# Cross-window attention on one core: an order of work kept as strings, single PSUM banks, and most products on GpSimd in halves

## The chip, the core and the metric

The kernel runs on one core of one Trainium2 chip. Times are device microseconds of that core for one launch. A core has five engines that run side by side, each with its own queue of instructions taken strictly in order: TensorE (PE, matmuls; PEld is its loading of weights), VectorE (DVE), ScalarE (ACT, here the exponentials), GpSimd (POOL) and SyncE (SP, here the queue that starts the transfers). They meet through semaphores. TensorE writes only to PSUM, which has eight banks of 512 fp32 columns over 128 partitions.

## The reference

A picture of 224 x 224 positions with 96 channels is projected to queries, keys and values. The first 48 channels attend within horizontal stripes of 8 rows, the other 48 within vertical stripes of 8 columns; each stripe has 1792 positions. The two results are put side by side and projected.

```python
qkv = jnp.einsum('bhwc,cd->bhwd', x, wqkv)          # x: 1,224,224,96; C2 = 48
q, k, v = qkv[..., :C], qkv[..., C:2*C], qkv[..., 2*C:]
qh, kh, vh = (t[..., :C2].reshape(28, 8*224, C2) for t in (q, k, v))
ah = softmax(einsum('bqc,bkc->bqk', qh, kh) * C2**-0.5)
oh = einsum('bqk,bkc->bqc', ah, vh)
# the same for t[..., C2:], with stripes of 8 columns: ov
out = einsum('bhwc,cd->bhwd', concat(oh, ov), wo)
```

So there are 56 stripes, each with a score matrix of 1792 x 1792, all of which goes through an exponential.

## The kernel before, in words

**Pairs of stripes.** The 56 stripes are worked two at a time: 28 pairs P, 14 of horizontal and then 14 of vertical ones (`NPH`). The two stripes of a pair (`w`) lie in the two halves of the partitions. Queries come in four chunks of columns (`CH`: 512, 512, 512, 256), keys in 14 tiles of 128. A *unit* is one key tile (two for the last chunk) against one chunk of queries, for both stripes: two banks of scores, 128 x 1024. A pair has 49 units. There are 28 x 49 = 1372.

**Two ways to the exponential.** Of each chunk, `NDC` = 3, 2, 2, 2 units go through VectorE (`d_units`, 252) and the rest through ScalarE (`a_units`, 1120):
- ScalarE, line 773: one ACTIVATE with Exp over two banks, out to a buffer `PT` (eight of them); then PV matmuls (line 738) on `PT`.
- VectorE: line 801 brings the scores to int16 (`I_sb`, 128 x 1024 for a unit, two units to a buffer of 2048). For two units together, line 813 makes `U_sb` and line 815 `E_sb`, bit operations over 2048 columns. Line 820 multiplies `I_sb` and `U_sb` to `G_sb`, one instruction for each unit. The exponential is `E` + `G`, so such a unit has two PV steps, one on each. A product is made on VectorE, or on GpSimd where the planner chose that.

**The rest.** Line 518 projects queries and keys, lines 529 and 535 bring them to SBUF; line 547 (on GpSimd; line 546 on VectorE for the first pair) takes the mean off the keys; lines 573 and 578 make the values. After a chunk's last PV, line 702 copies its sum to `OT_sb`, lines 618 and 653 project it, lines 606 and 658 take the reciprocal, lines 625 and 662 divide. For vertical stripes line 666, on GpSimd, adds the horizontal stripes' part (`Ph_sb`), and line 675 stores on SyncE's queue, which also loads x (line 412) and stores the horizontal part (line 639).

**What sets the order.** The program is not written out: a planner (`Planner`) runs when the kernel is built. It has a list of queues (*streams*) for each engine and a price for each operation (`occ`, the time for which it holds the engine, and `lat`, the time to its result), and always places the operation that can start first by these prices, with a rule of its own for TensorE (`pick_pe`), which weighs score matmuls (mode `q`) against all others (mode `v`). `emit` then writes each engine's instructions in the placed order with waits on semaphores. On the chip only the order is fixed; when each starts is set by its waits. A *lock* keeps the planner from placing GpSimd's work and VectorE's operations 813, 815 and 820 at one time; it is a price in the plan and no wait on the chip.

**PSUM.** Three pairs of banks (0-1, 2-3, 4-5: `ring`) hold scores. Banks 6 and 7 (`obanks`) collect PV sums of the live chunks. Projections (`fill`) take a free bank of 6 and 7, or one half of a score pair (`FillPool`).

The few lines that tell how a product comes to GpSimd before:

```python
def choose(op):
    work = sum(o_.occ for q_ in (dve_ot, dve_d1, dve_ev) for o_ in q_ if all(...))
    for g in gs:
        if work >= WANT and pl.t["pool"] <= op.start + 1.0:
            g.eng, g.occ, g.lat = "pool", 2.12, 2.2
            pool_v.append(g)
```

Of the kernel before, what the change touches and what calls it, by code (L numbers as in the profile page):

```python
# [26 lines left out]

class Op:
    __slots__ = ("eng", "occ", "lat", "fn", "deps", "soft", "alloc", "then", "wait", "tok", "dma", "mode", "start", "end", "lock")

    def __init__(s, eng, occ, lat, fn, deps=(), soft=(), alloc=(), then=None, dma=None, mode=None):
        s.eng, s.occ, s.lat, s.fn, s.deps, s.soft, s.alloc, s.then = eng, occ, lat, fn, list(deps), list(soft), list(alloc), then
        s.wait = s.start = s.end = None
        s.tok, s.dma, s.mode, s.lock = {}, dma, mode, eng == "pool"
# [38 lines left out]
SWITCH = 0.10  # L73


class Planner:
# [21 lines left out]
    def ready(s, op):  # L98
        t = 0.0
        for d in op.deps:  # L100
            if d.end is None:
                return None
            if not (d.eng == "pe" and op.eng == "pe"):
                t = max(t, s.when(d, op.eng))
# [13 lines left out]
    def place(s, op, t):  # L118
        deps = list(op.deps)
        for pool, name, n in op.alloc:  # L120
            ks = pool.peek(lambda o: s.when(o, op.eng), n)[1]
            deps += pool.take(ks)
            op.tok[name] = ks[0] if n == 1 else sorted(ks)
# [26 lines left out]
    def n_q(s, t):  # L150
        return sum(1 for w, _ in s.ring.order(lambda o: s.when(o, "pe")) if w <= t + EPS)

    def pick_pe(s, cands):
        t = s.t["pe"]
        run_end = max(s.t["act"], t) + 0.903 * s.pend
        C = []
        for r, prio, q in cands:
            C.append((max(r, t + (SWITCH if q[0].mode != s.mode else 0.0)), prio, q))
        if any(c[1] == PRIO[0] for c in C) and run_end - t < DRUN:
            C = [c for c in C if c[1] != PRIO[1]]  # L160
        V = [c for c in C if c[2][0].mode == "v"]
        Q = [c for c in C if c[2][0].mode == "q"]
        now = t + EPS
        first = min(C, key=lambda c: (c[0], c[1]))
        if s.mode == "q":
            q_now = [c for c in Q if c[0] <= now]
            if q_now:
                return min(q_now, key=lambda c: c[1])
            v_now = [c for c in V if c[0] <= now + SWITCH]
            q_soon = [c for c in Q if c[0] <= t + HOLD]  # L170
            if q_soon:
                return min(q_soon, key=lambda c: c[0])
            if v_now:
                return min(v_now, key=lambda c: c[1])
            return first
        v_now = [c for c in V if c[0] <= now]
        q_now = [c for c in Q if c[0] <= t + SWITCH + EPS]
        need = SWITCH + 0.46
        if v_now:
            c = min(v_now, key=lambda c: c[1])  # L180
            if q_now:
                if t + c[2][0].occ > run_end - need:
                    return min(q_now, key=lambda c: c[1])
                if t > run_end - RUN and s.n_q(t + SWITCH) >= BATCH:
                    return min(q_now, key=lambda c: c[1])
            return c
        if q_now and (s.n_q(t + SWITCH) >= BATCH or t + 0.25 > run_end - need):
            return min(q_now, key=lambda c: c[1])
        return first

    def run(s):
        while True:
            best = None
            for e, streams in s.streams.items():
                cands = []
                for prio, q in streams:
                    if q:
                        r = s.ready(q[0])
                        if r is not None:
                            cands.append((r, prio, q))  # L200
                if not cands:
                    continue
                if e == "pe":
                    c = s.pick_pe(cands)
                else:
                    cands = [(max(r, s.t[e]), p, q) for r, p, q in cands]
                    m = min(c[0] for c in cands)
                    c = min((c for c in cands if c[0] <= m + 0.03), key=lambda c: c[1])
                if best is None or c[0] < best[0]:
                    best = c  # L210
            if best is None:
                break
            s.place(best[2].popleft(), best[0])
# [10 lines left out]
EPS, HOLD, RUN, BATCH = 0.05, 0.12, 1.2, 1  # L224
PRIO = (1, 0, 3, 5, 4, 2)
WANT = 0.8
NEAR, LEAD, SPACE, PACE, DRUN, FIRST = 1, 8, 3, 0.9, 1.0, 0


def bass_standalone__window_attn_cswin__vision_kernel(  # L230
# [27 lines left out]
    with es:  # L258
# [31 lines left out]
        def two(s):  # L290
            return ps3[:, 2 * s:2 * s + 2, :]
# [14 lines left out]
        dve_ot, dve_d1, dve_ev, dve_ts = (pl.stream("dve", i) for i in range(4))  # L306
# [3 lines left out]
        ring = Pool([0, 1, 2])  # L310
        obanks = Pool([6, 7])
        pl.ring = ring
# [4 lines left out]
        class FillPool:  # L317


            def __init__(s):  # L320
                s.pair, s.half = None, {}

            def peek(s, when, n):
                near = any(k.left <= NEAR for k in live) or len(live) != 1
                got = obanks.order(when)
                if got and not near:
                    return (got[0][0], [got[0][1]])
                opt = []
                for k, f in s.half.items():
                    if f is not None and all(o.end is not None for o in f):  # L330
                        opt.append((max([when(o) for o in f], default=0.0), k))
                if s.pair is None:
                    opt += [(t, 2 * p) for t, p in ring.order(when)]
                opt.sort()
                opt = opt or got
                return (opt[0][0], [opt[0][1]]) if opt else None

            def take(s, ks):
                k = ks[0]
                if k >= 6:  # L340
                    return obanks.take(ks)
                if s.pair is None:
                    s.pair = k // 2
                    deps = ring.take([s.pair])
                    s.half = {k: None, k ^ 1: deps}
                    return deps
                deps, s.half[k] = s.half[k], None
                return deps

            def free(s, k, by):  # L350
                if k >= 6:
                    obanks.free(k, by)
                    return
                s.half[k] = list(by)
                if s.half[k ^ 1] is not None:
                    ring.free(s.pair, s.half[k] + s.half[k ^ 1])
                    s.pair, s.half = None, {}
        fills = FillPool()
# [236 lines left out]
        def out_war(P):  # L595

            assert P < 2 or len(out_dma[P - 2]) == 8
            return out_dma[P - 2][-1:] if P >= 2 else []

        def fin(P, c):  # L600
# [7 lines left out]
            if is_h[P]:  # L608
                bcs = list(range(q0 // 64, (q0 + qs) // 64))
                for i in range(0, len(bcs), 4):  # L610
# [17 lines left out]
                    def rel(op, rop=rop):  # L628
# [3 lines left out]
                                   ("dve", 0.07 + 0.1 * n, d2, out_war(P), True, dve_ev, [], rel)], stream=pe_fin)  # L632
# [10 lines left out]
            else:  # L643
                for w in range(2):
# [28 lines left out]
                    def done(op, w=w, j=j, hold=hold):  # L673
# [9 lines left out]
                                   ("pool", 0.95, d3, out_dma[NPH - 2][-1:] + out_dma[NPH - 1][-1:] + out_war(P), False, pool_o, [], done)],  # L683
                                  stream=pe_fin)
                    hold += ops[:2]
                    fin_pe[P].append(p)
# [4 lines left out]
        def pv_done(k, op):  # L691
# [12 lines left out]
            def then(ev):  # L704
                obanks.free(k.bank, [ev])
# [7 lines left out]
        class OTPool:  # L713
# [3 lines left out]

            def peek(s, when, n):
# [4 lines left out]
                return obanks.peek(when, 1)  # L723

            def take(s, ks):
# [4 lines left out]
                return obanks.take(ks)  # L730

        def pv_op(k, kts, lhs, rhs, deps, then):
            q0, qs = CH[k.c]

            def fn(e):
                for i, kt in enumerate(kts):
                    for w in range(2):
                        ins = e.matmul(bank(k.bank)[64 * w:64 * w + 64, 0:qs], lhsT=lhs(w, kt), rhs=rhs(w, i, qs),  # L738
                                       start=(op.tok["first"] and i == 0), stop=(k.last is op and i == len(kts) - 1))
# [6 lines left out]
            op = Op("pe", 0.222, 0.40, fn, deps, [], [(OTPool(k), "o", 1)], placed, mode="v")  # L746
            return op

        def qk(e, u, s):
# [3 lines left out]
            for i, kt in enumerate(kts):  # L753
                for w in range(2):
                    ins = e.matmul(bank(2 * s + w)[:, i * qs:(i + 1) * qs], lhsT=KT_sb[b][64 * w:64 * w + C2, kt * 128:(kt + 1) * 128],  # L755
                                   rhs=QT_sb[b][64 * w:64 * w + C2, q0:q0 + qs], start=True, stop=True)
            return ins

        def add_a(i, u):
# [6 lines left out]
            q = Op("pe", 0.222, 0.40, None, [k_early[P] if kts[-1] < 2 else k_ready[P], q_ready[(P, c)]], [], [(ring, "s", 1)], q_then, mode="q")  # L766
            q.fn = lambda e: qk(e, u, q.tok["s"])
# [4 lines left out]
            a = Op("act", 0.903, 1.023, None, [q], [], [(pts, "p", 1)], act_then)  # L772
# [14 lines left out]
        n_d = [0]  # L787
        held = []

        def add_d(u, soft):  # L790
# [4 lines left out]
            q = Op("pe", 0.222, 0.40, None, [k_early[P] if kts[-1] < 2 else k_ready[P], q_ready[(P, c)]], soft, [(ring, "s", 1)], mode="q")  # L795
            q.fn = lambda e: qk(e, u, q.tok["s"])
# [153 lines left out]
```

## Time and profile before

| | before |
|---|---|
| median of 3 runs | 1052.47 us |
| lowest, highest | 1051.34, 1058.28 us |
| the profiled execution: its time | 1050.19 us |
| its span, first to last instruction | 1048.3 us |
| granted TensorE clock | 0.998 |
| exponentials on ScalarE (line 773) | 1120 |
| units on VectorE (line 801) | 252 |
| products on VectorE, on GpSimd (line 820) | 224, 28 |

The page of a profile gives busy time of each engine and its share of the span, the chain of work that ended last, and groups of instructions, with the mean time of one and the idle time of the engine ahead of them. For ScalarE and VectorE the time of one instruction counts from its dispatch, which can come while the one before still runs; the pace is then read from a row of the chain, which gives a stretch and how many instructions it holds. In a row of the timeline stand the start, the duration, the engine, the line, the operation, and in brackets the idle time ahead of it and what ended it.

### The profile page before, as it was taken

How to read it: one execution, taken by the hardware profiler on the slowest of the kernel's cores; microseconds unless marked ns; L12 is line 12 of the kernel's file. 1: busy time of each engine (PE TensorE's matmuls, PEld its weight loads, DVE VectorE, ACT ScalarE, POOL GpSimd, SP SyncE). 2: the span in 40 equal slices, each digit the busy share in tenths (PEclk: the TensorE clock that was granted, in tenths of full speed). 3: DMA queues.
4: the chain of work that ended last, by engine and by line, in shares of the span. 5: the costliest groups of instructions: out<-in, count | busy, mean ns of one | idle time of the engine just before them, and what ended most of it. 6: DMA issues, size and time to landing. Idle time of an engine off the chain costs nothing.

```text
span 1048.3 us, 25024 instructions
## 1 busy us (share of the span) xinstructions
PE 1021.6 (97%) x10602; PEld 383.7 (37%) x10602; DVE 964.5 (92%) x1772; ACT 1031.1 (98%) x1128; POOL 234.3 (22%) x171
## 2 busy tenths in 40 slices
PE   8999999999999999999999999999999999999997
PEld 2333333333333333333333333333333333333332
DVE  6999988999998989999999999999999999999896
ACT  6999999999999999999999999999999999999997
POOL 0211011000011100100114434343316323213352
PEclk9999999999999999999999999999999999999999
DMA  6133334342313334231542122122212212212011
GB/s 109 37 28 53 46 28 63 50 49 28 63 36 36 46 45 64 28 51 24 54 61 46 43 46 54 35 47 51 44 33 54 51 31 51 48 43 37 16 25 29
DMA packets 191368, 46.69 MB, mean 45 GB/s; under 512 B 191256, under 2 KB 191256, under 8 KB 191256
## 3 DMA queue, kind: packets, MB, share of 16 engines
q1 hardware_dynamic: 190664, 45.04, 27.1%
q8 instruction: 83, 1.36, 0.6%
q14 instruction: 29, 0.24, 0.1%
q10 hardware_dynamic: 592, 0.06, 0.0%
HBM read 0.10 MB, written 9.63 MB: 9 GB/s over the span
## 4 chain that ended last, share of the span: by engine, by line
ACT 97%; DVE 1%; PE 1%; DMA 0%; SPq 0%; issue 0%; ACTq 0%; POOL 0%; POOLq 0%; DVEq 0%
ACT PT L773 97%; DMA xT_sb<-in_x_dram 0%; PE ps L755 0%; SPq L421 0%; PE ps L738 0%; DVE KT_sb L535 0%; DVE V_sb L578 0%; SPq L412 0%; DVE I_sb L801 0%; DVE KT_sb L546 0%; ACTq L258 0%; POOL out_sb L666 0%; POOLq L258 0%; PE ps L653 0%; PE ps L518 0%
## 5 line engine op out<-in xcount | busy, mean ns | idle before, releaser
L773 ACT ACTIVATE PT<-ps 128x1024 bf16<-128x1024 f32 x1120 | 1027.5, 1271 | 2.7 <-PE ps L755 2.7
L755 PE MATMUL ps<-QT_sb,KT_sb 48*128 48x512 bf16 (+1 forms) x3136 | 476.7, 357 | 15.6 <-ACT PT L773 5.4
L738 PE MATMUL ps<-PT,V_sb 128*64 128x512 bf16 (+1 forms) x2520 | 394.9, 364 | 1.2 <-ACT PT L773 1.0
L801 DVE TENSOR_SCALAR I_sb<-ps 128x1024 int16<-128x1024 f32 x252 | 307.3, 1220 | 26.6 <-PE ps L755 24.7
L755 PEld LDWEIGHTS ps<-QT_sb,KT_sb 48*128 48x128 bf16 x3136 | 130.1, 93 | 357.9 <-ACT PT L773 273.6
L666 POOL TENSOR_TENSOR out_sb<-tmp,Ph_sb 112x384 bf16<-112x384 f32 x112 | 121.3, 1093 | 250.2 <-DVE tmp L662 235.0
L738 PEld LDWEIGHTS ps<-PT,V_sb 128*64 128x64 bf16 x2520 | 119.4, 108 | 129.0 <-issue 115.5
L820 DVE TENSOR_TENSOR G_sb<-I_sb,U_sb 128x1024 bf16<-128x1024 bf16 x224 | 163.9, 744 | 0.3
L547 POOL TENSOR_SCALAR KT_sb<-KT_sb,negmean 128x1792 bf16<-128x1792 bf16 x27 | 53.9, 1995 | 319.3 <-DVE kjunk L540 282.0
L820 POOL TENSOR_TENSOR G_sb<-I_sb,U_sb 128x1024 bf16<-128x1024 bf16 x28 | 59.3, 2122 | 241.9 <-DVE E_sb L815 241.9
L738 PE MATMUL ps<-G_sb,V_sb 128*64 128x512 bf16 (+1 forms) x616 | 97.3, 350 | 0.4 <-DVE G_sb L820 0.4
L738 PE MATMUL ps<-E_sb,V_sb 128*64 128x512 bf16 (+1 forms) x616 | 89.9, 351 | 0.8 <-DVE E_sb L815 0.2
L813 DVE TENSOR_SCALAR U_sb<-I_sb 128x2048 int16<-128x2048 int16 x126 | 88.1, 699 | 0.2
L815 DVE TENSOR_SCALAR E_sb<-I_sb 128x2048 int16<-128x2048 int16 x126 | 86.1, 683 | 0.0
L518 PE MATMUL ps<-xT_sb,w_sb 96*64 96x512 bf16 x448 | 79.8, 366 | 2.0 <-DMA xT_sb<-in_x_dram 1.5
L702 DVE CAST OT_sb<-ps 128x512 bf16<-128x512 f32 x112 | 69.3, 619 | 11.0 <-PE ps L738 10.6
L535 DVE TENSOR_SCALAR_CACHE_REDUCE KT_sb<-ps 128x512 bf16<-128x512 f32 x110 | 67.7, 619 | 12.0 <-PE ps L518 11.4
L529 DVE TENSOR_SCALAR QT_sb<-ps 128x512 bf16<-128x512 f32 x110 | 66.8, 616 | 7.4 <-PE ps L518 7.0
L662 DVE TENSOR_TENSOR tmp<-ps,rc 112x384 f32<-112x384 f32 x112 | 62.0, 554 | 1.9
L578 DVE CAST V_sb<-ps 128x480 bf16<-128x480 f32 (+1 forms) x112 | 55.6, 499 | 6.1 <-PE ps L573 6.0
L625 DVE TENSOR_TENSOR out_sb<-ps,rc 128x384 bf16<-128x384 f32 x98 | 54.2, 553 | 1.2
L573 PE MATMUL ps<-w_sb,xT_sb 96*64 96x48 bf16 x1568 | 43.9, 191 | 0.0
(32 smaller groups left out, 309.5 us busy)
## 6 DMA issues: line engine op xcount, KB each, us to landing
Ph_sb<-out_sb SPq DMA_DIRECT2D x112, 84.0 KB, 4.4
out_dram<-out_sb SPq DMA_DIRECT2D x112, 84.0 KB, 1.9
xT_sb<-in_x_dram SPq DMA_TRANSPOSE x254, 2.4
wo_sb<-in_wo_dram SPq DMA_DIRECT2D x4, 9.0 KB
wo_sb<-one_sb SPq DMA_DIRECT2D x4, 0.0 KB
w_sb<-in_wqkv_dram ACTq DMA_DIRECT2D x1, 54.0 KB, 3.4
xT_sb<-in_x_dram SPq DMA_DIRECT2D x2, 3.0 KB, 3.7
```

Of the source, the lines that this page charges most:

```text
L518: ins = e.matmul(bk[64 * w:64 * w + 64, 0:qs], lhsT=w_sb[0:C, wblk(P, kind), :], rhs=rhs, start=True, stop=True)
L529: return e.tensor_scalar(dst, src, A128, None, ALU.mult)
L535: return e.tensor_scalar(dst, src, 1.0, None, ALU.mult, ALU.add, accum_out=acc)
L666: return e.tensor_tensor(out_sb[b][0:HB, :, w, 2 * c:2 * c + 2, :].rearrange("p h d c -> p d h c"), tmp[hold[1].tok["t"]][0:HB, 0:n, :].re ...
L702: return e.tensor_copy(OT_sb[b][:, q0:q0 + qs], bk[:, 0:qs])
L738: ins = e.matmul(bank(k.bank)[64 * w:64 * w + 64, 0:qs], lhsT=lhs(w, kt), rhs=rhs(w, i, qs), start=(op.tok["first"] and i == 0), stop=(k.l ...
L755: ins = e.matmul(bank(2 * s + w)[:, i * qs:(i + 1) * qs], lhsT=KT_sb[b][64 * w:64 * w + C2, kt * 128:(kt + 1) * 128], rhs=QT_sb[b][64 * w: ...
L773: a.fn = lambda e: e.activation(PT[a.tok["p"]][:].rearrange("p (s n) -> p s n", s=2), two(q.tok["s"]), ACTF.Exp, scale=LN128)
L801: d.fn = lambda e: e.tensor_scalar(I_sb[d0.tok["y"]][:, j * 1024:(j + 1) * 1024].rearrange("p (s n) -> p s n", s=2), two(q.tok["s"]), 128. ...
L813: f.fn = lambda e: e.tensor_scalar(U_sb[y()][:, :], I_sb[y()][:, :], M_FRAC, HALF, ALU.bitwise_and, ALU.bitwise_or)
L815: x2.fn = lambda e: e.tensor_scalar(E_sb[x2.tok["l"]][:, :], I_sb[y()][:, :], M_EXP, E_LOW, ALU.bitwise_and, ALU.bitwise_or)
L820: g.fn = lambda e, i0=i0, i1=i1: e.tensor_tensor(G_sb[x2.tok["l"]][:, i0:i1], I_sb[y()][:, i0:i1].bitcast(BF16), U_sb[y()][:, i0:i1].bitca ...
```

## The change

The planner's own choices of order, of banks and of products for GpSimd go, and five strings, `PLAN`, take their place. `pe`, `dve` and `pool` name, for each instruction of TensorE, VectorE and GpSimd, the queue that is served next (`forced`). For TensorE: 0 warming up, 1 scores for ScalarE, 2 scores for VectorE, 3 PV of `E` and `G`, 4 PV of `PT`, 5 projections of results, 6 projections of x. For VectorE: 0 set-up, 1 copies of line 702, 2 line 801, 3 other copies and divisions, 4 lines 813, 815 and 820. For GpSimd: 1 key updates, 2 products, 3 additions. `far` has one bit for each product: 1 sends it to GpSimd, as two halves of 512 columns. `bank` says where each result goes in PSUM: a digit is a bank; scores take that bank and the next, all else the one bank. All eight banks lie in one pool. ScalarE and SyncE are planned as before.

The strings' counts: `pe` 3560 characters (18 zeros, 1120 ones, 252 twos, 504 threes, 1120 fours, 210 fives, 336 sixes), `dve` 1464, `pool` 535 (27 ones, 396 twos, 112 threes), `far` 252 (198 ones), `bank` 2030. The planner's prices still tell when it places what, but no longer the order within these three engines. Also changed: the prices of the exponential and of a change of mode, and an addition or a division that follows stores now waits for all eight of them (`late`). Code for fused score and PV matmuls (`place2`, `weave`) and for line 801 in halves (`HALVES`) is there and isn't reached: no string holds w, x, y or z, and `HALVES` is False.

```diff
+PLAN = {
+    "pe": (
+        "00000000000000000066666666111662641421461411423613412641341261341431641166331441254144124163134164411363315414"
...
+    "far": (
+        "11110111101111111110100101110011101010111111111011101001011001111111111111111110011110110111110110111011101111"
...
-SWITCH = 0.10
+SWITCH = {"q": 0.122, "v": 0.097}
+ACT = 0.9165
...
-    def pick_pe(s, cands):
...
+    def far(s, op):
+        return next(s.bits) == "1"
+
+    def forced(s, e):
+        i = s.at[e]
+        code = PLAN[e]
+        if i >= len(code):
+            return None
+        c = code[i]
...
+            q = s.streams[e][int(c)][1]
...
+        r = s.ready(q[0])
...
+        t = s.t[e]
+        if e == "pe":
+            m = "q" if c in FUSE else q[0].mode
+            if m != s.mode:
+                t += SWITCH[m]
+        return (max(r, r2, t), 0, q, q2)
...
-        ring = Pool([0, 1, 2])
-        obanks = Pool([6, 7])
-        pl.ring = ring
+        banks = Pool(range(8))
...
-        class FillPool:
...
+        class Home:
+
+            def __init__(s, digits, each):
+                s.digits, s.each = digits, each
 
             def peek(s, when, n):
...
+                at = pl.bank + pl.ahead
+                ks = [int(d) + i for d in PLAN["bank"][at:at + s.digits] for i in range(s.each)]
...
+        ring, singles, fills = Home(1, 2), Home(2, 1), Home(1, 1)
...
-            return out_dma[P - 2][-1:] if P >= 2 else []
+            return lambda: [] if P < 2 else out_dma[P - 2] if len(out_dma[P - 2]) == 8 else None
...
-            for i0, i1 in ((0, 1024), (1024, 2048)):
-                g = Op("dve", 0.62, 0.70, None, [f, x2])
...
+            def product(i0, i1, occ, deps):
+                g = Op("dve", occ, occ + 0.08, None, deps)
+                g.fn = lambda e: e.tensor_tensor(G_sb[x2.tok["l"]][:, i0:i1], I_sb[y()][:, i0:i1].bitcast(BF16),
+                                                 U_sb[y()][:, i0:i1].bitcast(BF16), ALU.mult)
                 g.lock = True
-                gs.append(g)
+                return g
+            los = [product(1024 * i, 1024 * i + 512, 1.09, [f, x2]) for i in range(2)]
+            gs = [product(1024 * i, 1024 * i + 1024, 0.62, [f, x2]) for i in range(2)]
...
-                    if work >= WANT and pl.t["pool"] <= op.start + 1.0:
-                        work -= WANT
-                        g.eng, g.occ, g.lat = "pool", 2.12, 2.2
-                        pool_v.append(g)
-                        n_d[0] += 1
+                    if pl.far(op):
+                        g.fn = product(1024 * i + 512, 1024 * i + 1024, 1.09, []).fn
+                        for o_ in (lo, g):
+                            o_.eng, o_.occ, o_.lat = "pool", 1.09, 1.15
+                            pool_v.append(o_)
                     else:
                         near.append(g)
```

## The prediction

> **What bounds the kernel now.** I read the page first, from the busy times to the chain, then the groups, then the waits of ScalarE, then stretches of the timeline.
>
> ```profile
> span 1048.3 us, 25024 instructions
> PE 1021.6 (97%) x10602; PEld 383.7 (37%) x10602; DVE 964.5 (92%) x1772; ACT 1031.1 (98%) x1128; POOL 234.3 (22%) x171
> ACT 97%; DVE 1%; PE 1%; DMA 0%; SPq 0%; issue 0%; ACTq 0%; POOL 0%; POOLq 0%; DVEq 0%
> ```
>
> Three engines look full, but the chain that ends last is ScalarE for 97%. The chain in order of time gives the pace:
>
> ```profile
> 18.33 156.87 ACT PT L773 x171
> 176.33 574.86 ACT PT L773 x627
> 753.80 56.94 ACT PT L773 x62
> 810.75 229.33 ACT PT L773 x250
> ```
>
> 627 exponentials follow each other in 574.86 us; without the first one's own 1.02 that is 573.84/626 = 0.9167 us each, and the last row gives 228.31/249 = 0.9169. The group's mean of 1271 ns is longer only because one instruction is dispatched while the one before still runs. So the kernel has a floor: first exponential at 12.67, its 1.02, then 1119 x 0.9167 = 1025.8, which ends at 1039.5. The last one really ends at 1041.92, and 6.4 us of closing work follow (PV, copy, projection, division, add, store). The order of work can recover only 1041.9 - 1039.5 = 2.4 us, whatever it frees on other engines. Where these 2.4 us lie is shown by ScalarE's rows at the start and by its waits:
>
> ```profile
> 12.67 1.02 ACT L773 ACTIVATE PT<-ps 128x1024 bf16<-128x1024 f32 x1 [0.90 <-PE ps L755]
> 14.18 3.77 ACT L773 ACTIVATE PT<-ps 128x1024 bf16<-128x1024 f32 x4 [0.49 <-PE ps L755]
> 18.33 12.02 ACT L773 ACTIVATE PT<-ps 128x1024 bf16<-128x1024 f32 x13 [0.37 <-PE ps L755]
> ```
>
> ```profile
> ACT PT L773 <- PE ps L755: 2.7, 6, 0.9
> ```
>
> The second exponential could have begun one pace later, at 12.67 + 0.92 = 13.59, and begins at 14.18 (0.59 late); the sixth is 0.48 late; in the chain there are gaps near 175 and 752, worth 0.3 and 0.9. All end with the score matmuls of line 755. 1% of this kernel's time is 10.5 us, about what a measurement tells from no change; the whole reserve is a quarter of that.
>
> **The change, part by part.**
>
> *Number of exponentials.* Each character of the order string names the queue that is served next. TensorE's string holds 1120 times the queue of ScalarE's scores, 252 times that of VectorE's. Both counts are those of before (x1120 and x252 of lines 773 and 801). The floor above stays: 0.
>
> *Products from VectorE to GpSimd.* The string of bits has 198 ones; GpSimd's string has 396 products (two halves each), 27 key updates, 112 additions. Before, GpSimd made 28, so 170 products move.
>
> ```profile
> L801 DVE TENSOR_SCALAR I_sb<-ps 128x1024 int16<-128x1024 f32 x252 | 307.3, 1220 | 26.6 <-PE ps L755 24.7
> L666 POOL TENSOR_TENSOR out_sb<-tmp,Ph_sb 112x384 bf16<-112x384 f32 x112 | 121.3, 1093 | 250.2 <-DVE tmp L662 235.0
> L820 DVE TENSOR_TENSOR G_sb<-I_sb,U_sb 128x1024 bf16<-128x1024 bf16 x224 | 163.9, 744 | 0.3
> L547 POOL TENSOR_SCALAR KT_sb<-KT_sb,negmean 128x1792 bf16<-128x1792 bf16 x27 | 53.9, 1995 | 319.3 <-DVE kjunk L540 282.0
> L820 POOL TENSOR_TENSOR G_sb<-I_sb,U_sb 128x1024 bf16<-128x1024 bf16 x28 | 59.3, 2122 | 241.9 <-DVE E_sb L815 241.9
> ```
>
> VectorE loses 170 x 163.9/224 = 124 us: 964.5 to about 840, 80% of the span. GpSimd loses 59.3 and gets 396 halves. A half (512 columns) is not in this trace: not under 2122/2 = 1.06 us, and, with the undisturbed addition of 384 columns (0.91) and the 1024 columns (2.12) on one line, at most 0.91 + 128 x 1.21/640 = 1.15 us. I take 1.09, nearer to the product's own row: 432 us, GpSimd about 607 us (595 to 630), 58%. On the path this is worth 0, since neither engine is the bound; the cover is VectorE's 20% idle time. The Trainium skill, "GPSIMD Engine Reference", section 3.1, puts a two-input operation at about 2.6 cycles an element at 1.2 GHz, estimated 1.11 us for a half and 440 us in all; this trace has 2122/1024 = 2.07 ns, 2.5 cycles. The same page advises VectorE for such products; here the slower engine is the idle one.
>
> *The port that both share.* A price could lie here, and the trace shows it:
>
> ```profile
> 723.49 2.66 POOL L666 TENSOR_TENSOR out_sb<-tmp,Ph_sb 112x384 bf16<-112x384 f32 x2
> 723.98 1.40 DVE L813 TENSOR_SCALAR U_sb<-I_sb 128x2048 int16<-128x2048 int16 x1
> 176.20 2.12 POOL L820 TENSOR_TENSOR G_sb<-I_sb,U_sb 128x1024 bf16<-128x1024 bf16 x1 [1.51 <-DVE E_sb L815]
> 177.16 1.70 DVE L820 TENSOR_TENSOR G_sb<-I_sb,U_sb 128x1024 bf16<-128x1024 bf16 x1
> ```
>
> The product on VectorE that began 0.96 after GpSimd's took 1.70 and not 0.66: it ended 0.55 after GpSimd's end (178.32), as if it had begun only then. So the SBUF-only operations of the two engines (lines 813, 815, 820 against all of GpSimd's) exclude each other for whole instructions. Busy time of this shared thing before: 28 x 2.12 + 27 x 1.76 + 112 x 0.91 (undisturbed) + 476 x 0.68 = 533 us; after: 432 + 149 + 306 x 0.68 = 789 us, 75%. The additions all lie in the second half (524 us), where it is 192 x 1.09 + 12 x 1.76 + 112 x 0.91 + 153 x 0.68 = 436 us, 83%. If the two engines met at random, each of VectorE's 306 operations would find GpSimd busy in 581/1048 = 55% of cases and wait half a half, 0.55 us: 93 us, VectorE about 933 of 1048, still less than now. Halves keep a single wait under 1.1 us; a whole product, up to 2.1. Against a buffer of this length stands the reserve of a score pair: with three pairs of banks a pair is due two exponentials later, 1.83 us, and needs 0.39 for its matmuls and some 0.06 for the signal, so it may be 1.4 us late at no cost. Price on the path: 0, if a wait is one instruction; if the cover is gone, what exceeds 1.4 us (rival 2).
>
> *The order on TensorE.* The work is the same; only changes between score matmuls (128 columns wide) and the rest cost more. I counted 1932 in the trace of before and 1966 in the string; the timeline has up to 0.23 us of "issue" ahead of the weights at such a change, so that is at most 34 x 0.23 = 8 us more on an engine that waits 273.6 us for ScalarE ahead of line 755: 0. At the start the string has eight projections, then three score pairs at once, into banks 0-1, 2-3 and 5-6, and only then the rest of the projections; before, it was one score pair, VectorE's pair, a projection, then the next. The second exponential then finds its scores, the sixth too by the string: -1.1. The first one waits for the keys' update on VectorE (line 546), whose order is the same: 12.67 stays. The gaps at 175 and 752 come where projections and PV of 2 us are queued ahead of scores; I take -1.1 for these, bounds 0 to -1.3.
>
> *Eight single banks.* Scores still lie in two neighbouring banks, now also from odd banks (304 of 1372 pairs begin at 1, 3 or 5). No row shows a pair across the old borders; all pairs of before run at 0.917 wherever they lie and whatever else runs, so 0; I set no bound beside this, since nothing in the trace has an exponential's end more than 3 ns off one pace after the end before it, except those that waited.
>
> *Waits added.* Divisions and additions wait for all eight stores of an earlier stripe, not the last; these count on one semaphore, in order: 0. Additions are queued behind halves on GpSimd (up to 4.4 us later), and behind the additions the stores on SyncE, and behind these the loads of x. Loads are issued a stripe (37 us) ahead: 0.
>
> *New gaps.* An order fixed in advance can be late where the chip differs from the plan. I take +0.5 (0 to 10). Sum: -1.1 - 1.1 + 0.5 = -1.7 on the path: span 1046.6, time 1050.19 - 1.7 = 1048.5 for an execution as the profiled one (1.9 lie around the span). The median of the runs shown is 2.3 above it (1052.47), so I say **1050.8** for a median.
>
> **Rivals.**
> 1. *As many gaps as before.* The fixed order loses 2 to 3 us in other places, for instance where VectorE waits for the port. For it: 1.5 times the use of the port; against: VectorE has 120 us more room. Time 1052.5, the change +0.
> 2. *Slower, by the port.* If VectorE, once it waits, gets in only behind a run of GpSimd's instructions and not between two, a wait goes up to four halves, 4.4 us, on average 2.2, which is 0.8 beyond the reserve of 1.4; behind it are the drains of line 801, so banks, so scores. Both products of a pair go to GpSimd in 76 of the 126 pairs, and its run fills 4.4 of 8.3 us: 76 x 0.53 x 0.8 = 32 us, time 1084; if one such wait in three reaches ScalarE, 1063. It decides from where waits exceed 1.4 us. Against it: at 723.98 VectorE's operation waited with two additions in a row on GpSimd, and ended 0.55 after the first one's end; the second was held back (2.66 for two of 0.91). They took turns. By the Trainium skill, "SBUF — State Buffer", section "SBUF: two separate sides", the one that starts first holds the pair for its whole instruction and the other fully blocks; it doesn't say who is next, and the rows above do.
> 3. *A late product at the head of TensorE's queue.* PV of a product is placed by plan; TensorE takes nothing past it. If 20 of 198 come late by 0.6 beyond the reserve, +12: 1064.
> 4. *Faster by over 1%* would take an earlier first exponential or a shorter end by 8 us; nothing in the diff touches them.
>
> **How the numbers follow.** Forecast 0.5, rival 1 0.33, rivals 2 and 3 in full 0.13, rival 4 0.02, gaps in between (+3 to +10) 0.02. Faster by over 1%: 0.02; slower by over 1% (over 1063): 0.12; within: 0.86. The range goes from 1046.5 (all gaps gone, on the profiled execution, and a shorter end) to 1061 (rivals 2 and 3 in their small form); inside it the forecast's own is 1048 to 1053.
>
> **What would show it.** Right: 1120 exponentials in a row at 0.917 from 12.7, ScalarE's wait for line 755 under 1.5 us, VectorE about 840 us, GpSimd about 600, halves of 1.06 to 1.15, no VectorE operation of lines for U, E and G much over 1.8. Wrong: stretches of the chain that leave ScalarE, a pace other than 0.917, or U and E of 3 us and more.

## The result, and the profile after

The changed kernel takes 1060.81 us in the median of 17 runs (1054.93 to 1067.33), the kernel before 1052.36 in the runs beside it (17, 1050.46 to 1059.36). The ratio is 1.0061 with a 95% interval of 1.0042 to 1.0080: slower by 0.6% (the two medians alone differ by 0.8%), where 0.2% faster was forecast. The profiled execution has a span of 1056.5 us, 8.2 more than before, at a time of 1058.33. First the page of the kernel after: span, busy times, the granted clock in 40 slices, and the chain by engine.

```profile
span 1056.5 us, 25283 instructions
PE 1024.0 (97%) x10602; PEld 388.0 (37%) x10602; DVE 899.2 (85%) x1602; ACT 1033.2 (98%) x1128; POOL 612.1 (58%) x539
PEclk9999999999999999999999999999999989999998
ACT 82%; PE 11%; DVE 6%; issue 1%; DMA 0%; SPq 0%; ACTq 0%; POOL 0%; POOLq 0%; DVEq 0%
```

The chain, 97% ScalarE before, has 11% of TensorE and 6% of VectorE in it: ScalarE now waits. And the row of the clock has an 8 in the 33rd slice, which before had only nines there. The groups that answer to those shown of before:

```profile
L981 POOL TENSOR_TENSOR G_sb<-I_sb,U_sb 128x512 bf16<-128x512 bf16 x396 | 457.1, 1181 | 373.8 <-DVE E_sb L977 359.1
L975 DVE TENSOR_SCALAR U_sb<-I_sb 128x2048 int16<-128x2048 int16 x126 | 101.2, 803 | 1.2
L977 DVE TENSOR_SCALAR E_sb<-I_sb 128x2048 int16<-128x2048 int16 x126 | 93.7, 744 | 0.0
L981 DVE TENSOR_TENSOR G_sb<-I_sb,U_sb 128x1024 bf16<-128x1024 bf16 x54 | 46.2, 861 | 0.2
```

The number of exponentials is the same, and so is their pace: from the end of one to the end of the next the median is 0.917 us, as before. The 1120 took 8.1 us longer, and 7.2 of this are gaps: 18 of them, 9.7 us in all, against 7 and 2.5 before. The other 0.9 is a mean of 0.9175 between the gaps, against 0.9167; the same order in a later run (below, kept busy at the start) has 0.9167, so this belongs to the one execution. ScalarE's waits for the scores, 2.7 us in all before, now read:

```profile
ACT PT L925 <- PE ps L903: 8.4, 13, 1.6
```

Of the 9.7 us, 6.3 lie between 857 and 873. What happens there is seen in rows of the timeline of the kernel after, here put in order of time for GpSimd, VectorE, TensorE and ScalarE:

```profile
852.21 4.49 POOL L981 TENSOR_TENSOR G_sb<-I_sb,U_sb 128x512 bf16<-128x512 bf16 x4
854.50 2.75 DVE L975 TENSOR_SCALAR U_sb<-I_sb 128x2048 int16<-128x2048 int16 x1
857.17 0.68 DVE L977 TENSOR_SCALAR E_sb<-I_sb 128x2048 int16<-128x2048 int16 x1
857.78 0.68 DVE L819 CAST OT_sb<-ps 128x512 bf16<-128x512 f32 x1
858.51 0.36 PE L768 MATMUL ps<-wo_sb,OT_sb 128*64 128x97 bf16 x8 [1.90 <-DVE OT_sb L819]
859.24 1.94 ACT L925 ACTIVATE PT<-ps 128x1024 bf16<-128x1024 f32 x2 [1.60 <-PE ps L903]
```

GpSimd runs four halves in a row until 856.70. VectorE's `U` is dispatched at 854.50, during the third, and ends 0.55 after the fourth: it took 2.75 us in place of 0.69. `E` and the copy of line 819 stand behind it, TensorE's projection of line 768 waits 1.90 for that copy with the next scores behind it, and ScalarE stands still. The same place by stretches of 3.41 us (busy time of PE, PEld, DVE, ACT and POOL, each with its instructions, then the granted clock):

```profile
853.16:856.57 3.41, 3.41 (x48) 1.59 (x46) 3.41 (x4) 3.41 (x5) 3.41 (x4) 1.00 0.19 42
856.57:859.99 3.42, 1.52 (x32) 0.99 (x30) 3.32 (x9) 1.82 (x3) 2.18 (x3) 1.00 0.24 48
859.99:863.40 3.41, 3.41 (x24) 1.15 (x20) 2.10 (x3) 2.21 (x3) 3.41 (x5) 0.50 0.25 50
863.40:866.81 3.41, 3.41 (x20) 0.79 (x16) 2.20 (x4) 2.27 (x3) 0.76 (x1) 0.50 0.20 39
866.81:870.23 3.42, 3.42 (x20) 1.19 (x18) 1.63 (x4) 2.12 (x3) 0.00 (x0) 0.50 0.41 84
870.23:873.64 3.41, 3.41 (x26) 0.81 (x22) 2.44 (x5) 3.26 (x4) 3.24 (x3) 1.00 0.19 38
```

After one stretch in which TensorE was busy for 1.52 of 3.42 us, its clock is granted at 0.50 for exactly three stretches, 10.24 us. Exponentials then start 1.54 us apart (861.99, 863.52, 865.06) in place of 0.92, so a first gap of 1.7 us turns into 6.3 in all.

Single executions differ by such stretches, and the mean granted clock of each goes with their number: of the 17, two are at 0.997 (1055 us), six at 0.992 to 0.994 (1057 to 1058), eight at 0.987 to 0.989 (1060.8 to 1063), one at 0.981 (1067). A stretch of 10.24 us at half clock lowers the mean by 10.24 x 0.5/1056 = 0.005.

### The profile page after: what moved, and what is told of

It reads as the page before. It is cut to its first block, busy times and chain, and to the rows that moved or that the text cites. A ratio compares the mean times of both kernels' runs of the same rounds, so it can differ in the third digit from the quotient of the medians.

```text
span 1056.5 us, 25283 instructions
## 1 busy us (share of the span) xinstructions
PE 1024.0 (97%) x10602; PEld 388.0 (37%) x10602; DVE 899.2 (85%) x1602; ACT 1033.2 (98%) x1128; POOL 612.1 (58%) x539
## 4 chain that ended last, share of the span: by engine, by line
ACT 82%; PE 11%; DVE 6%; issue 1%; DMA 0%; SPq 0%; ACTq 0%; POOL 0%; POOLq 0%; DVEq 0%
ACT PT L925 82%; PE ps L903 5%; PE ps L856 5%; DVE I_sb L963 2%; DVE E_sb L977 1%; PE ps L633 1%; DVE U_sb L975 1%; DMA xT_sb<-in_x_dram 0%; PE ps L768 0%; DVE OT_sb L819 0%; DVE G_sb L981 0%; DVE tmp L777 0%; SPq L536 0%; DVE V_sb L693 0%; DVE KT_sb L650 0%
## 5 line engine op out<-in xcount | busy, mean ns | idle before, releaser
L981 POOL TENSOR_TENSOR G_sb<-I_sb,U_sb 128x512 bf16<-128x512 bf16 x396 | 457.1, 1181 | 373.8 <-DVE E_sb L977 359.1
L856 PE MATMUL ps<-PT,V_sb 128*64 128x512 bf16 (+1 forms) x2520 | 399.0, 367 | 1.0 <-ACT PT L925 0.8
L781 POOL TENSOR_TENSOR out_sb<-tmp,Ph_sb 112x384 bf16<-112x384 f32 x112 | 106.6, 970 | 44.5 <-DVE tmp L777 33.2
L975 DVE TENSOR_SCALAR U_sb<-I_sb 128x2048 int16<-128x2048 int16 x126 | 101.2, 803 | 1.2
L977 DVE TENSOR_SCALAR E_sb<-I_sb 128x2048 int16<-128x2048 int16 x126 | 93.7, 744 | 0.0
L856 PE MATMUL ps<-E_sb,V_sb 128*64 128x512 bf16 (+1 forms) x616 | 92.1, 351 | 1.0 <-DVE E_sb L977 0.6
L633 PE MATMUL ps<-xT_sb,w_sb 96*64 96x512 bf16 x448 | 82.5, 370 | 2.9 <-DMA xT_sb<-in_x_dram 1.2
L662 POOL TENSOR_SCALAR KT_sb<-KT_sb,negmean 128x1792 bf16<-128x1792 bf16 x27 | 50.6, 1873 | 23.4 <-DVE kjunk L655 19.1
L981 DVE TENSOR_TENSOR G_sb<-I_sb,U_sb 128x1024 bf16<-128x1024 bf16 x54 | 46.2, 861 | 0.2
```

The costliest lines, as they stand in the source:

```text
L633: ins = e.matmul(bk[64 * w:64 * w + 64, 0:qs], lhsT=w_sb[0:C, wblk(P, kind), :], rhs=rhs, start=True, stop=True)
L781: return e.tensor_tensor(out_sb[b][0:HB, :, w, 2 * c:2 * c + 2, :].rearrange("p h d c -> p d h c"), tmp[hold[1].tok["t"]][0:HB, 0:n, :].re ...
L856: return e.matmul(bank(k.bank)[64 * w:64 * w + 64, x0:x1], lhsT=lhs(w, kts[i])[p0:p1], rhs=rhs(w, i, qs)[p0:p1, x0:x1], start=(op.tok["fir ...
L975: f.fn = lambda e: e.tensor_scalar(U_sb[y()][:, :], I_sb[y()][:, :], M_FRAC, HALF, ALU.bitwise_and, ALU.bitwise_or)
L977: x2.fn = lambda e: e.tensor_scalar(E_sb[x2.tok["l"]][:, :], I_sb[y()][:, :], M_EXP, E_LOW, ALU.bitwise_and, ALU.bitwise_or)
L981: g.fn = lambda e: e.tensor_tensor(G_sb[x2.tok["l"]][:, i0:i1], I_sb[y()][:, i0:i1].bitcast(BF16), U_sb[y()][:, i0:i1].bitcast(BF16), ALU. ...
```

## The experiments

Theory 1: the turns that the plan gives GpSimd and VectorE on the port they share are not kept on the chip; VectorE comes late, TensorE stands still, the clock halves. Rival A: the fixed order and the banks are too tight, whatever GpSimd does. Rival B: the halves are too long on GpSimd. The first four kernels ran on one chip, beside a median of 1051.55 for the kernel before.

**Halves of 16 columns.**

```diff
+            def product(i0, i1, occ, deps, thin=False):
+                i1 = i0 + 16 if thin else i1
...
+                        g.fn = product(1024 * i + 512, 1024 * i + 1024, 1.09, [], True).fn
+                        lo.fn = product(1024 * i, 1024 * i + 512, 1.09, [], True).fn
```

> The kernel after, with its order and banks, but each half of a product on GpSimd covers 16 columns in place of 512 (the other columns of G stay zero), so GpSimd's 396 instructions and their use of the shared port nearly vanish. Theory 1 (the plan's turns on the port that GpSimd and VectorE share are not kept on the chip; VectorE's operation waits for one half more than planned, TensorE stands still behind it, and where that lasts some 2 us the granted clock halves for 10.24 us): no gaps on ScalarE, no stretch at half clock before the end, span 1046 to 1048, time 1048 to 1050. Rival A (the fixed order and the banks are too tight for the chip, whatever GpSimd does): gaps and dips stay, 1055 to 1062.

G is set to zero once at the start, and most of what GpSimd's products add is left out of the result. Measured: 1054.97 in the median, which neither theory forecast; but the 12 executions go from 1048.0 to 1058.0, and those at a mean clock of 0.999 take 1048.0 to 1048.3. The profiled one is of these: span 1046.5, one gap (0.74) after the first exponential. So the order and the banks are sound, and rival A falls for the body of the kernel; but something else lowers the clock in nine of twelve executions.

**Turns bound by semaphores.**

```diff
+        if op.lock:
+            if s.port is not None and s.port.eng != op.eng:
+                deps.append(s.port)
+            s.port = op
```

> The kernel after, with one thing added: an operation that uses the shared port waits on a semaphore for the operation of the other engine that the plan puts ahead of it on that port, so that the planned turns are kept. All products are made. Theory 1: the waits of two halves go, gaps under 2 us in all, few or no dips of the clock, time 1049 to 1053. Rival A: no change, 1055 to 1062. Rival B (it is not who goes first, but that 1.15 us for each half on GpSimd is more than the order bears): no change or slower, 1057 to 1065.

Measured: 1058.83 (1050.45 to 1062.97), the best at mean clocks of 0.999 and 0.997 at 1050.5 and 1050.7, the others at 0.983 to 0.991. The median missed the forecast of theory 1 and lies in the ranges of rivals A and B. No operation of VectorE waits for the port any more. The profiled execution (1062.97) shows another cause; its stretches from the start on:

```profile
4.23:7.64 3.41, 3.17 (x16) 1.12 (x14) 0.41 (x1) 0.20 (x1) 0.00 (x0) 1.00 1.06 159
7.64:11.06 3.42, 1.39 (x40) 1.14 (x42) 1.10 (x6) 1.32 (x5) 0.00 (x0) 1.00 1.21 173
11.06:24.71 13.65, 13.00 (x86) 3.15 (x80) 9.21 (x17) 9.50 (x11) 4.48 (x4) 0.50 0.49 96
24.71:38.36 13.65, 13.65 (x58) 2.70 (x56) 7.45 (x15) 9.11 (x9) 6.25 (x5) 0.50 0.00 0
38.36:45.00 6.64, 6.58 (x72) 2.23 (x68) 5.78 (x10) 6.39 (x7) 2.26 (x2) 1.00 0.01 2
```

While TensorE waits for x it is busy for 1.39 of 3.42 us, and its clock is halved from 11.06 to 38.36, 27.3 us, although it is busy for all but 0.65 of these. This costs ScalarE 9.4 us in fifteen gaps up to 40 us. Such a stretch near the start is called the early stretch below. Another 1.08 us gap near 507 is followed by a stretch of 6.83 at half clock.

**The same products in the greedy order, pairs of banks.**

```diff
+                    if next(bits) == "1":
+                        i0, i1 = (0, 1024) if g is gs[0] else (1024, 2048)
+                        lo = product(i0, i0 + 512)
+                        g.fn = product(i0 + 512, i1).fn
...
+                            o_.eng, o_.occ, o_.lat = "pool", 1.12, 1.2
```

> The kernel before with its own planner and its banks in pairs, and the same 198 products on GpSimd in halves (the bits of the kernel after); additions wait for all eight stores as in the kernel after. This is the move of the products alone, without the searched order. Theory 1: the greedy order spreads VectorE's and GpSimd's turns without a search and has as many reversed turns; gaps of 10 us and more and some dips, 1058 to 1075. Rival A: the products are harmless by themselves, 1050 to 1054.

Measured: 1080.36 (1079.01 to 1081.93), ratio 1.0254 (1.0224 to 1.0284), above both forecasts. Without the searched order the products cost 2.5%, in 57 gaps (31 us in the profile). The largest gap stands behind this operation on VectorE:

```profile
1022.29 4.48 POOL L821 TENSOR_TENSOR G_sb<-I_sb,U_sb 128x512 bf16<-128x512 bf16 x4
1023.18 4.14 DVE L815 TENSOR_SCALAR U_sb<-I_sb 128x2048 int16<-128x2048 int16 x1
1028.87 1.02 ACT L774 ACTIVATE PT<-ps 128x1024 bf16<-128x1024 f32 x1 [3.40 <-PE ps L756]
```

`U` is dispatched during the first of four halves and ends 0.55 after the last: it was passed over three times. How many of the other gaps are turns on the port and how many the greedy choice itself, this run does not tell apart.

**One late VectorE operation, four times.**

```diff
+LATE = ((8, 1), (12, 1), (16, 1), (20, 1))
...
+                if (P, c) in LATE:
+                    for i in range(4):
+                        e.tensor_copy(junk[:, i, 0:qs], bk[:, 0:qs])
```

> The kernel before, with VectorE held for four copies of 512 columns (about 2.4 us in all) ahead of the copy of line 702 in four places (pairs 8, 12, 16 and 20, second chunk). This measures what one late VectorE operation costs, and whether the clock answers. Theory 1: each place costs ScalarE up to 1 us by itself and in most executions 3 to 4 us more by a stretch of 10.24 us at half clock, so 1058 to 1072, with the granted clock at 0.98 to 0.99 and single executions 3 to 4 us apart. Rival C (the dips of the kernel after come from something else, such as the density of its matmuls): clock stays at 0.998, time 1052.5 to 1056.

Measured: 1070.45 (1063.61 to 1074.26), ratio 1.0147 (1.0107 to 1.0186), mean clocks 0.976 to 0.990. In the profiled execution all four places are followed by a stretch at half clock, of 3.41, 10.24, 3.41 and 6.83 us; the second place:

```profile
488.14:491.56 3.42, 1.58 (x18) 0.51 (x16) 3.42 (x7) 2.48 (x3) 0.00 (x0) 1.00 0.00 0
491.56:494.97 3.41, 3.41 (x26) 1.11 (x26) 2.92 (x7) 1.97 (x2) 0.00 (x0) 0.50 0.00 0
```

The four places cost ScalarE 3.1, 5.6, 3.4 and 4.1 us in gaps, for 2.4 us of VectorE each. This execution has the early stretch too (half clock from 13.69 to 37.58, 8.9 us of gaps), so its time is not that of the four places alone. Rival C falls: an otherwise unchanged kernel has a dip at each of the four places.

Over the six profiles of before, after and these four, and the six below, the middle of the kernel has 13 stretches (of 3.41 us, in step with the changes of the clock) in which TensorE was busy for less than 73%; 12 of them were followed at once by half clock, one of 63% was not. None of those at 74% or more was. In the first 15 and the last 12 us the busy share does not decide: ten stretches of 63 to 73% there were not followed by half clock, while three at the start, of 41, 72 and 75%, were.

The next four, on one chip (before: 1051.51), keep TensorE busy at the start with matmuls that nobody reads:

```diff
-        "000000000000000000666666661116626...
+        "0000000000000000006600000006666660001116626...
...
-        for i in range(NWARM):
+        for i in range(NWARM + 10):
```

> The kernel after with ten idle matmuls (of the kind of its 18 warming-up ones, into a bank not yet in use) at its start: seven behind the second projection, where TensorE waits 1.2 to 2.3 us for x, and three ahead of the first scores. Theory 2 (after the projections TensorE is so little busy in one 3.41 us window that the clock halves, in most executions of the searched order, for some 20 to 27 us, and ScalarE starves at 1.54 us an exponential): this early stretch goes; left are the gaps and single dips in the middle, 1055 to 1058.5, against 1060.8 for the kernel after. Rival D (the lower mean clock of single executions comes from dips in the middle alone): 1060 to 1062, mean clocks down to 0.987 as before.

> The ten idle matmuls at the start and the binding of the turns on the shared port together, all products made. Theories 1 and 2 together: nearly all executions at 1050 to 1053, median 1050.5 to 1051.5, mean clock 0.997 to 0.999. If the early stretch is not the cause (rival D): 1057 to 1060, as with the binding alone.

> The kernel before with seven idle matmuls behind its second projection. Theory 2: the executions of before at 1056 to 1058 (mean clock 0.985 to 0.989) come from the same early stretch and go; median 1050 to 1051.5, spread under 3 us. Rival D: 1051.5 with single ones at 1056 to 1058.

> The searched order and single banks, products on GpSimd cut to 16 columns a half (the other columns of G stay zero), with the ten idle matmuls at the start. Theory 2: all executions at 1048 to 1049, against 1048 to 1058 without them; so order and banks by themselves bring the 2 us that the sum of the prediction had. Rival D: 1048 to 1058 as before, median 1055.

| | median, us | range | ratio to before |
|---|---|---|---|
| after, kept busy at the start | 1054.55 | 1053.59 to 1057.48 | 1.0028 (1.0006 to 1.0050) |
| the same, turns bound | 1052.86 | 1049.85 to 1055.18 | 1.0000 (0.9976 to 1.0025) |
| before, kept busy at the start | 1051.17 | 1050.42 to 1051.66 | 0.9976 (0.9951 to 1.0000) |
| after, halves of 16 columns, kept busy | 1048.51 | 1047.80 to 1048.96 | 0.9960 (0.9939 to 0.9981) |

Theory 2 holds in that no execution of these four kernels is at a mean clock under 0.993, so none has a stretch of 20 us or more; the spread of the last two shrinks to 1.2 us, and the median of the kernel after is 6.3 lower. That one is 0.4 under its range, the last two are as forecast (one execution 0.2 below), and the bound kernel is above its forecast of 1050.5 to 1051.5. Its VectorE waits show a part of why:

```profile
DVE U_sb L980 <- POOL G_sb L986: 16.1, 28, 1.2
DVE G_sb L986 <- POOL G_sb L986: 11.4, 19, 1.2
```

Bound both ways, VectorE stands still for halves that come late themselves, up to 1.2 us; one such wait, of 1.23, is followed by a gap of 1.08 near 500. In this profile 1.6 of the 4.2 us of gaps lie from 384 to 390, around its one stretch at half clock (386.15 to 389.57); what holds TensorE up there is open. This led to the last pair (before: 1051.01), in which only GpSimd waits:

```diff
+        if op.lock:
+            if op.eng == "dve":
+                s.port = op
+            elif s.port is not None:
+                deps.append(s.port)
```

> The kernel after with the ten idle matmuls at the start and the turns on the shared port bound one way only: an operation of GpSimd waits for the operation of VectorE that the plan puts ahead of it, but VectorE waits for none of GpSimd's. With the binding both ways VectorE stood still up to 1.2 us for a half that came late. Theory 1, refined (what costs is VectorE's lateness, whether a port or a semaphore holds it): no VectorE operation of lines for U, E and G waits longer than one half, gaps 1 to 3 us, median 1049 to 1051, so faster than both kernels. Rival B (the products' own time on GpSimd is too long for the order, so TensorE waits for products once VectorE goes first): 1053 to 1058.

> The kernel before with seven idle matmuls at its start and the same one-way binding for its 28 products, 27 key updates and 112 additions on GpSimd. Its gaps of 0.3 and 0.9 us near 175 and 752 lie behind VectorE operations; if these were held by the port, they go: 1050 to 1050.8 against 1051.2 with the idle matmuls alone. If they come from the greedy order itself, 1051 to 1051.5.

Measured: 1047.40 (1046.99 to 1048.45), ratio 0.9957 (0.9939 to 0.9976): 0.4% faster than the kernel before, with all products made, and below the forecast of 1049 to 1051. Rival B falls. Page and waits of ScalarE of this kernel:

```profile
ACT 98%; PE 1%; DVE 0%; ACTq 0%; POOL 0%; POOLq 0%; issue 0%
L931 ACT ACTIVATE PT<-ps 128x1024 bf16<-128x1024 f32 x1120 | 1026.8, 1218 | 0.9 <-PE ps L909 0.9
```

The one idle stretch of 0.9 is ahead of the first exponential: 1120 follow each other without a gap. 43 operations of VectorE still wait for the port, 18 us in all, but none past one instruction. The kernel before with the same binding: 1050.92 (0.9985; 0.9965 to 1.0004), which lies between its two forecasts. Its gaps near 177 and 753 stay, and no operation of VectorE just ahead of them waited for the port, so they belong to the greedy order. Its profiled execution still has a short stretch at half clock at the start (15.63 to 19.05), in spite of the idle matmuls.

## Why the prediction was wrong, by its steps

**The floor: right.** 1120 exponentials at 0.917 us, nothing on ScalarE changed. With no gaps the span is 1045.5 (one-way binding), where the sum had 1046.6 with 0.5 of new gaps; the rest is a first exponential at 12.34 and not 12.67.

**Order and banks, -2.2: right.** With the products' time on GpSimd taken away and both kernels busy at the start, 1048.51 - 1051.17 = -2.7; some 0.9 of this is an earlier first exponential (12.51 against 13.37 in the two profiles). Without idle matmuls, at full clock, the two profiled executions differ by 1048.34 - 1050.19 = -1.9. The gaps at 14, 18, 175 and 752 are gone, and one of 0.7 is new; pairs of scores over other borders of banks run at the same pace.

**The products, 0 on the path with +0.5 of new gaps: the first step that failed, by size.** 1054.55 - 1048.51 = +6.0, inside its bounds of 0 to 10. GpSimd's own price was near: 612 us against 607, a half 1.15 undisturbed against 1.09, at a pace of 4.49/4 = 1.12 in a row. VectorE is busy 899 and not 840. With halves of 16 columns it is 873, so 33 of the 59 are not due to the halves: the sum took 170 times 0.73 us off, but the row counts from dispatch, and from one end to the next a product takes 0.60. Of the other 26, 22 lie in the longer rows of `U` and `E`. What failed was the cover. The waits are no random ones: 56 operations waited 31 us in all, a third of the estimate of 93. But the reserve of 1.4 us was read from three pairs of banks in the greedy order; in the searched order, at 854, `U` was 2.06 late and ScalarE 1.7, so some 0.4 us was left. And "they took turns", read from one row, holds for 54 of the 56 waits; two were passed over once, and one of these made the gap at 857.63. In the profile of the same order kept busy at the start the same two are passed over, and the first costs 3.3 us, with 3.41 at half clock. In the greedy order one `U` was passed over three times. Rival 2 had the place and the mechanism, but its waits behind a run of halves were to be common; they were rare, and dear through the clock. That binding the turns, on GpSimd's side alone, takes the products' whole price away (1047.40, no gaps) shows that the turns are the cause. Who gets the port next, and why, is open.

**The clock: the step that was missing.** The row of the granted clock of before had nothing but nines over the body, and I took full speed as given. Keeping TensorE busy at the start takes 1060.81 - 1054.55 = 6.3 us off the median (5.4, each taken against before beside it), some 0.5 of it by an earlier first exponential (12.23 against 12.70); the rest is put down to half clock at the start. A part of the 6.0 is dips in the middle. The profiled execution of the kernel after has no early stretch; that others do is inferred from their mean clocks and from what the idle matmuls change. The kernel before has it as well (single executions at 1056 to 1058 with mean clocks of 0.985 to 0.989, 13 of the 35 beside the second four kernels), only less often; its own median loses 0.3. Why the searched order meets it more often is open: in the profiles of before and after, both without it, TensorE is busy for 3.60 and 3.88 of the 6 us from 8 to 14.

The Trainium skill, "TensorE: Matmul & The Clock Gate", Part 1, tells of a free-running window of 3413 ns and of half clock after an idle one; the trace agrees in the length (10.24 = 3 x 3.413). It differs in the condition: that part of the Trainium skill warns of idle gaps of over 3.4 us, while here 1.90 us were enough. By that condition the 2.75 us of `U` would have cost the first gap alone, 1.7 us; it cost 6.3.

**The chances.** Slower by over 1% did not come, within 1% did, and the 1060.81 lies at the upper end of the range, which was there for rivals 2 and 3; the sign was wrong. It was so because 0.33 for "as many gaps" left out that each gap may be followed by a stretch at half clock.

## What to carry to other kernels

A plan that keeps two engines apart on a shared resource only by its prices is no order: bind the turn by a semaphore, and only on the engine with time to spare, here GpSimd (1047.4 us, against 1052.9 bound both ways). With only 28 products, in the kernel before, the same binding brought nothing that can be told from noise. Where TensorE feeds an engine that is full to 97%, price a delay not by its own length but by what the clock does after it: look at TensorE's busy share per 3.4 us, at the start too. And compare executions by their mean clock before the medians.

## What the runs showed of the hardware that I had not expected

- TensorE's clock was granted at 0.50 for whole multiples of 3.41 us (one, two, three, seven and eight were seen). In the middle of the kernel this began right after a stretch in which TensorE was busy for 33 to 72%, not only after an idle one.
- At half clock TensorE was busy for 77 to 100% of each stretch, and stayed there for up to 27.3 us at the start, and for 3.4 to 10.2 in the middle. What ends it is open.
- VectorE, waiting for the port, mostly got it after the one GpSimd instruction that ran, but not always (two of 56 waits in the kernel after; in the greedy order one wait of 4.14 us, behind four halves).
- Ten matmuls that nobody reads, in 2 to 3 us of waiting at the start, went with a median lower by 6.3 us.
